# Attention before a routed MLP: three float32 key tiles per pair of heads instead of four

## The chip, the core and the metric

The kernel runs on one core of a Trainium2 chip. A core has TensorE (PE, matrix products; its weight loads are shown as PEld), VectorE (DVE), ScalarE (ACT), GpSimd (POOL) and SyncE (SP, which issues DMAs), each with its own instruction stream; they meet in semaphores. The metric is the time of one execution in microseconds; the median of three timed runs of the kernel before is 759.37 us (758.96 to 760.9).

## What is computed

Four batches of eight heads attend over 1152 keys with head size 64; the queries are first averaged in pairs, so there are 576 per head. The result goes through a routed MLP with eight experts (one per token, with a rule that keeps the previous token's expert for some tokens).

```python
q_pool = q.reshape(B, H, S // 2, 2, D).mean(axis=3)          # 4, 8, 576, 64
scores = scale * np.matmul(q_pool, k.transpose(0, 1, 3, 2))
attn = np.exp(scores - np.max(scores, axis=-1, keepdims=True))
attn = attn / (np.sum(attn, axis=-1, keepdims=True) + 1e-09)
x = np.matmul(attn, v)                                       # then the heads side by side
e = argmax(x[b, s] @ w_gate)  # or the token's before, where the local gate says so
out[b, s] = softmax(x[b, s] @ w_gate)[e] * (np.maximum(x[b, s] @ w1[e], 0.0) @ w2[e])
```

Everything is float32 from outside. Inside, most products are made of float16 or bfloat16 high and low parts.

## The kernel before

**Steps.** The 32 heads form 16 pairs (here numbered 0 to 15). A head has nine key tiles of 128 keys, so a pair has 18 steps; step `s` of the kernel is head `s // 9`, key tile `kt = s % 9`. The main loop in `attention` runs once per step and issues, in this order: `scores(s)` (four matmuls and, on ScalarE, the exponential into `PHI`, float32), `feed_max` (one or two units that compute the row maxima of the next head: matmuls into PSUM tiles tagged `m`, of which there are two, and a VectorE reduction, L199), one pending preparation operation of a later pair (`prep_ops`), at even steps `low(s // 2 - 1)`, and then `av(s - 6)`, since `LAG` is 6. So the value product of step 4 of a pair is issued in step 10 of the same pair.

**The value product.** `av(s)` multiplies the exponentials of one key tile with the values. For most tiles it takes three float16/bfloat16 products for each of five query blocks (L263 to L265): the top half of the float32 exponential (`top`, a bfloat16 view) with the high and with the low part of the values, and the low part of the exponential (`PLO`) with the high part of the values: 15 matmuls. For key tiles 4 and 8 (`F32K`) of each head it multiplies float32 with float32 instead (L261), five matmuls in the program, ten records in the trace, and needs no low part.

**Low parts.** `low(g)` computes `PLO` for two steps: POOL subtracts for the even step, VectorE for the odd one (L237). It leaves out the float32 tiles. POOL therefore makes the low parts of steps 0, 2, 6, 10, 12, 14 and 16 of a pair and VectorE those of 1, 3, 5, 7, 9, 11 and 15.

**Value tiles.** `VT` holds high part, a column of ones and low part in float16 for the seven tiles that are not float32; `VX` holds the two float32 tiles. `o6` makes the high parts with two ScalarE operations (L159, four tiles and three tiles for both heads), `o7` the low parts with two POOL operations (L162).

**What else runs in these steps.** From step 30 on, every 14 steps a piece of the experts' weights is loaded, converted by ScalarE and split by VectorE (`extra`; the split, L510, comes at steps 40, 54, 68 and so on). After every fourth pair a batch is finished; its router's many small VectorE operations come mainly in the steps of pairs 6, 10 and 14. After a head's last value product, ScalarE scales the result (L1171, L1165) and POOL subtracts once more (L1168, `xr`). All engines work through their own instructions in the order of the program. The order is the one in which the loop above issues them.

## Time and profile before

| | us |
|---|---|
| timed runs, median (lowest, highest) | 759.37 (758.96, 760.9) |
| the profiled execution | 763.41 |
| its span, first to last instruction | 761.4 |
| TensorE busy | 697.4 (92%) |
| VectorE busy | 620.5 (81%) |
| GpSimd busy | 503.4 (66%) |
| ScalarE busy | 477.0 (63%) |

The attention steps run from about 25 to 460 us, the experts after that. Busy shares are means over stages that have different limits, so what a change in the attention steps is worth has to be read in those steps: which engine waits for which there, and for how long. A timeline's row gives start, duration, engine, line and operation; a bracket at its end says how long the engine was idle before it and what it had waited for. A row of windows gives, for each stretch, how much of it each engine was busy, the granted share of TensorE's clock, and what the DMAs moved.

### The profile page before, as it was taken

What the parts mean: (1) busy time and instruction counts of PE and PEld (TensorE: products, weight loads), DVE (VectorE), ACT (ScalarE), POOL (GpSimd) and SP (SyncE); (2) the same over time, 40 slices, a digit from 0 to 9 for tenths busy, and PEclk for the clock granted to TensorE, in tenths of its full rate; (3) what the DMA queues carried; (4) which work ended last, traced back from release to release, by engine and by line L of the source; (5) the groups of instructions that cost most, each with busy time, mean ns of one, the idle gap of its engine ahead of it and who ended that gap; (6) DMA issues with size and microseconds to landing.
All of it is one profiled execution on the core that took longest, in us unless ns stands there. A gap on an engine that the chain in (4) does not pass through costs nothing. (4 is left out here: it accounts for less than half of the span.)

```text
span 761.4 us, 25799 instructions
## 1 busy us (share of the span) xinstructions
PE 697.4 (92%) x10664; PEld 611.1 (80%) x10664; DVE 620.5 (81%) x1098; ACT 477.0 (63%) x971; POOL 503.4 (66%) x456
## 2 busy tenths in 40 slices
PE   3899999999999999889999998888898999999994
PEld 0487788887778877778887887888897889999994
DVE  7778888888888888888888976689889899798851
ACT  2475777677477667567766655686767675565521
POOL 6575687778367767458666435853647567777776
PEclk9999999999899999999999999999999999999998
DMA  7363643586363586354593226696828884474411
GB/s 241 97 180 121 186 119 109 160 212 154 140 187 81 166 192 169 112 174 102 153 202 72 72 31 173 219 308 214 286 93 280 279 288 165 148 230 145 127 40 32
DMA packets 90058, 122.99 MB, mean 162 GB/s; under 512 B 40552, under 2 KB 46828, under 8 KB 89936
## 3 DMA queue, kind: packets, MB, share of 16 engines
q1 hardware_dynamic: 85152, 110.41, 49.8%
q0 software_dynamic: 4784, 10.86, 4.3%
q8 instruction: 87, 1.43, 0.8%
q14 instruction: 35, 0.29, 0.1%
HBM read 79.29 MB, written 16.85 MB: 126 GB/s over the span
## 5 line engine op out<-in xcount | busy, mean ns | idle before, releaser
L227 ACT ACTIVATE ph<-sc 128x576 f32<-128x576 f32 x288 | 187.6, 652 | 118.3 <-PE sc L225 99.8
L199 DVE TENSOR_REDUCE mx<-psm 128x1 f32<-128x512 f32 (+1 forms) x300 | 193.7, 662 | 57.2 <-PE psm L197 54.9
L237 POOL TENSOR_TENSOR pl<-ph 128x576 f16<-128x576 f32 x112 | 150.2, 1342 | 43.5 <-ACT ph L227 43.5
L934 DVE COPY wc<-w 128x2048 f16 x184 | 154.4, 839 | 26.7 <-PE pso L1069 22.6
L1061 PEld LDWEIGHTS <-wc 128*128 128x128 f16 x2208 | 126.1, 98 | 20.8 <-DVE wc L934 12.1
L264 PE MATMUL av<-vt,ph 128*128 128x64 f16 x1120 | 126.9, 196 | 0.0
L263 PE MATMUL av<-vt,ph 128*128 128x65 f16 x1120 | 126.4, 193 | 0.0
L265 PE MATMUL av<-vt,pl 128*128 128x65 f16 x1120 | 126.1, 192 | 0.0
L1069 PE MATMUL pso<-wc,hq 128*128 128x128 f16 x2208 | 123.4, 219 | 0.0
L1069 PEld LDWEIGHTS <-hq 128*128 128x128 f16 x2208 | 123.3, 98 | 0.0
L264 PEld LDWEIGHTS <-ph 128*128 128x128 bf16 x1120 | 104.9, 98 | 20.1 <-issue 0.5
L1073 POOL DMA_INDIRECT out<-ob,sid x92 | 100.6, 1093 | 30.9 <-issue 18.0
L225 PE MATMUL sc<-qa,ks 65*128 65x288 f16 (+1 forms) x576 | 119.9, 290 | 0.3 <-ACT qa L213 0.3
L263 PEld LDWEIGHTS <-ph 128*128 128x128 bf16 x1120 | 106.2, 98 | 17.2 <-issue 9.6
L223 PE MATMUL sc<-qs,ks 128*128 128x288 f16 x576 | 119.7, 290 | 0.2 <-ACT ph L227 0.2
L237 DVE TENSOR_TENSOR pl<-ph 128x576 f16<-128x576 f32 x112 | 106.3, 949 | 1.9 <-ACT ph L227 1.9
L265 PEld LDWEIGHTS <-pl 128*128 128x128 f16 x1120 | 105.3, 100 | 0.0
L508 POOL TENSOR_TENSOR w<-wf,w 128x512 f16<-128x512 f32 x48 | 62.8, 1315 | 53.4 <-ACT w L501 52.9
L197 PE MATMUL psm<-ks,qs 128*128 128x512 f16 x248 | 91.1, 387 | 6.6 <-DVE mx L199 6.1
L261 PEld LDWEIGHTS av<-vx,ph 128*128 128x128 f32 x640 | 82.1, 194 | 8.6 <-issue 5.1
L1168 POOL TENSOR_TENSOR xr<-xf,xr 128x320 f16<-128x320 f32 x30 | 33.2, 1106 | 77.1 <-ACT xr L1165 77.1
L1061 PE MATMUL psh<-xr,wc 128*128 128x128 f16 x1248 | 76.1, 221 | 8.7 <-DVE wc L934 5.8
(201 smaller groups left out, 1112.5 us busy)
## 6 DMA issues: line engine op xcount, KB each, us to landing
wf<-wq SPq DMA_DIRECT2D x128, 256.0 KB
qf<-qeo SPq DMA_DIRECT2D x16, 576.0 KB
vf<-vL SPq DMA_DIRECT2D x16, 576.0 KB
ks<-kd SPq DMA_DIRECT2D x32, 288.0 KB
kf<-kT SPq DMA_DIRECT2D x15, 576.0 KB
xts<-xr SPq DMA_DIRECT2D x23, 256.0 KB
qs<-qh SPq DMA_DIRECT2D x64, 72.0 KB
ks<-kl SPq DMA_DIRECT2D x32, 144.0 KB
```

Of the source, the lines that this page charges most:

```text
L199: V.tensor_reduce(out=mx[:, i, c:c + 1], in_=m[:, 0:w], op=ALU.max, axis=AX.X)
L223: T.matmul(sc[:, c, 0:288], ksl, QS[p][:, j, c * 288:(c + 1) * 288], start=True, stop=False)
L225: T.matmul(sc[:, c, 0:288], kal, QA[p % 3][u, j, c * 288:(c + 1) * 288], start=False, stop=True)
L227: A.activation(out=PHI[g % NPH][:, r * Q:(r + 1) * Q].rearrange("p (c q) -> p c q", c=2), in_=sc[:, :, 0:288], func=AF.Exp, scale=1.0 / 16)
L237: x.tensor_tensor(out=PLO[g % NPH][:, r * Q:r * Q + Q], in0=pf, in1=top(pf), op=ALU.subtract)
L263: T.matmul(o, ph[:, c:c + 128], v[:, j, kv, 0:65], start=(kt == 0 and t == 0), stop=False, skip_group_check=True)
L264: T.matmul(o[:, 0:64], ph[:, c:c + 128], v[:, j, kv, 65:129], start=False, stop=False, skip_group_check=True)
L265: T.matmul(o, pl[:, c:c + 128], v[:, j, kv, 0:65], start=False, stop=(kt == NKT - 1 and t == 4), skip_group_check=True)
L934: self.nc.vector.tensor_copy(w, self.W[ph % 2][:, bass.ds(self.ej[j], 1), :].rearrange("p o f -> p (o f)"))
L1061: self.nc.tensor.matmul(p[:, ft], w[:, ws, kk, ft * 128:ft * 128 + 128], x[:, 2 * kk + xs_], start=(n == 0 and ft == 0), stop=(n == 11 and ...
L1069: self.nc.tensor.matmul(p, h(hs, ft), w[:, ws, ft], start=(n == 0), stop=(n == 23))
L1073: sc = self.nc.gpsimd.indirect_dma_start(out=self.out.rearrange("b s (q d) -> (b s q) d", q=4), in_=o, in_offset=None, bounds_check=NTOK * ...
```

## The change

`FK` lists, for the first and the second head of a pair, which key tiles are float32: only tile 8 for the first, 4 and 8 for the second. So tile 4 of the first head (step 4 of each pair) is multiplied in float16, in 15 matmuls. Its low part is due at an even step and is thus made by POOL. `VT` holds eight tiles instead of seven, all that can be float16 in either head; `o6` converts the eight in one operation, and the second operation of `o7` covers four tiles instead of three. `VX` and its loads stay as they are.

```diff
--- before.py
+++ after.py
@@ -24,6 +24,7 @@
 LEAD = 4
 SHD = 3
 F32K = (4, 8)
+FK = ((8,), (4, 8))
 PREP0 = 13
 
 ONES = 0.007826805114746094
@@ -46,8 +47,7 @@
     KSA = [pers.tile([128, 2, 2, S], F16, name=f"ks{i}") for i in (1, 2, 0)]
     KSA = KSA[2:] + KSA[:2]
     QA = [pers.tile([128, 2, Q], F16, name=f"qa{i}") for i in range(3)]
-
-    VT = [lat.tile([128, 2, NKT - 2, 130], F16, name=f"vt{i}") for i in range(3)]
+    VT = [lat.tile([128, 2, NKT - 1, 130], F16, name=f"vt{i}") for i in range(3)]
     VX = [lat.tile([128, 2, 2, 65], F32, name=f"vx{i}") for i in range(2)]
     QD = [pers.tile([128, 128], F16, name=f"qd{i}") for i in range(3)]
     MN = [pers.tile([128, 5, 65 - 64 * i], F16, name=f"mn{i}") for i in range(2)]
@@ -151,12 +151,11 @@
                 r = slice(64 * j, 64 * j + 64)
                 SP.dma_start(out=QA[i][r, j], in_=ql[r])
 
-        vk = [vf.rearrange("p h (t d) -> p h t d", d=D)[:, :, k] for k in (slice(0, 4), slice(5, 8))]
-        tk = [VT[i][:, :, k] for k in (slice(0, 4), slice(4, 7))]
+        vk = [vf.rearrange("p h (t d) -> p h t d", d=D)[:, :, k] for k in (slice(0, 4), slice(4, 8))]
+        tk = [VT[i][:, :, k] for k in (slice(0, 4), slice(4, 8))]
 
         def o6():
-            for x, v in zip(tk, vk):
-                A.activation(out=x[:, :, :, 0:64], in_=v, func=AF.Copy)
+            A.activation(out=VT[i][:, :, :, 0:64], in_=vf.rearrange("p h (t d) -> p h t d", d=D)[:, :, 0:8], func=AF.Copy)
 
         def o7(g):
             G.tensor_tensor(out=tk[g][:, :, :, 65:129], in0=vk[g], in1=tk[g][:, :, :, 0:64], op=ALU.subtract)
@@ -232,7 +231,8 @@
 
     def low(g):
         for r, x in enumerate((G, V)):
-            if (2 * g + r) % NKT not in F32K:
+            n, kt = divmod(2 * g + r, NKT)
+            if kt not in FK[n % 2]:
                 pf = PHI[g % NPH][:, r * Q:r * Q + Q]
                 x.tensor_tensor(out=PLO[g % NPH][:, r * Q:r * Q + Q], in0=pf, in1=top(pf), op=ALU.subtract)
 
@@ -253,16 +253,16 @@
             AV[n] = ps_a.tile([128, 512], F32, name="av", tag="av")
         a = AV[n]
         ph, pl = top(PHI[s // 2 % NPH]), PLO[s // 2 % NPH]
-        v, kv = VT[p % 3], kt - (kt > F32K[0])
+        v = VT[p % 3]
         for t in range(5):
             o = a[:, t * 65:t * 65 + 65]
             c = (s % 2) * Q + t * 128
-            if kt in F32K:
+            if kt in FK[j]:
                 T.matmul(o, PHI[s // 2 % NPH][:, c:c + 128], VX[p % 2][:, j, F32K.index(kt)], start=False, stop=(kt == NKT - 1 and t == 4), skip_group_check=True)
                 continue
-            T.matmul(o, ph[:, c:c + 128], v[:, j, kv, 0:65], start=(kt == 0 and t == 0), stop=False, skip_group_check=True)
-            T.matmul(o[:, 0:64], ph[:, c:c + 128], v[:, j, kv, 65:129], start=False, stop=False, skip_group_check=True)
-            T.matmul(o, pl[:, c:c + 128], v[:, j, kv, 0:65], start=False, stop=(kt == NKT - 1 and t == 4), skip_group_check=True)
+            T.matmul(o, ph[:, c:c + 128], v[:, j, kt, 0:65], start=(kt == 0 and t == 0), stop=False, skip_group_check=True)
+            T.matmul(o[:, 0:64], ph[:, c:c + 128], v[:, j, kt, 65:129], start=False, stop=False, skip_group_check=True)
+            T.matmul(o, pl[:, c:c + 128], v[:, j, kt, 0:65], start=False, stop=(kt == NKT - 1 and t == 4), skip_group_check=True)
         if kt == NKT - 1:
             x = emit_x(n, AV.pop(n), ps_m, wide)
             later.extend(x[0])
```

GpSimd's order around the second pair's first steps, before (L237 is `low`, L1168 the subtraction behind a finished head, L162 the low part of the values, L126 the next pair's queries):

```order
L237 TENSOR_TENSOR pl_153<-ph_148 128x576
L1168 TENSOR_TENSOR xr<-xf,xr 128x5x64
L162 TENSOR_TENSOR vt_136<-vf,vt_136 128x2x3x64
L237 TENSOR_TENSOR pl_149<-ph_144 128x576
L237 TENSOR_TENSOR pl_151<-ph_146 128x576
L1168 TENSOR_TENSOR xr<-xf,xr 128x5x64
L237 TENSOR_TENSOR pl_153<-ph_148 128x576
L126 TENSOR_TENSOR qf<-qf_859 128x576
```

and now (the lines of `prep_ops` have moved up by one in the file):

```order
L237 TENSOR_TENSOR pl_153<-ph_148 128x576
L1168 TENSOR_TENSOR xr<-xf,xr 128x5x64
L161 TENSOR_TENSOR vt_136<-vf,vt_136 128x2x4x64
L237 TENSOR_TENSOR pl_149<-ph_144 128x576
L237 TENSOR_TENSOR pl_150<-ph_145 128x576
L237 TENSOR_TENSOR pl_151<-ph_146 128x576
L1168 TENSOR_TENSOR xr<-xf,xr 128x5x64
L237 TENSOR_TENSOR pl_153<-ph_148 128x576
```

The low part of step 4 (`pl_150`) stands between those of steps 2 and 6, ahead of the head's `xr`.

TensorE's order at step 10 of the same pair, before (L197 is a unit of the maxima, L223 the next step's scores):

```order
L197 LDWEIGHTS qs
L197 MATMUL psm<-ks_129,qs 128x512
L261 MATMUL av<-vx_138,ph_145 128x65 x5
L223 LDWEIGHTS ks_128
L223 MATMUL sc<-qs,ks_128 128x288
```

and the end of the same place now, the last two of five query blocks:

```order
L263 LDWEIGHTS ph_145
L263 MATMUL av<-vt_135,ph_145 128x65
L264 LDWEIGHTS ph_145
L264 MATMUL av<-vt_135,ph_145 128x64
L265 LDWEIGHTS pl_150
L265 MATMUL av<-vt_135,pl_150 128x65
L263 LDWEIGHTS ph_145
L263 MATMUL av<-vt_135,ph_145 128x65
L264 LDWEIGHTS ph_145
L264 MATMUL av<-vt_135,ph_145 128x64
L265 LDWEIGHTS pl_150
L265 MATMUL av<-vt_135,pl_150 128x65
```

In place of five float32 products stand 15 pairs of weight load and matmul, and the first L265 of them waits for POOL's `pl_150`.

## Rows read from the trace of the kernel before

**Rows 1.** Timeline of TensorE, pair 3: start us, us, engine line operation.

```profile
118.33 0.41 PE L223 MATMUL sc<-qs,ks 128*128 128x288 f16 x2
...
119.04 0.19 PE L263 MATMUL av<-vt,ph 128*128 128x65 f16 x1
...
119.50 0.41 PE L223 MATMUL sc<-qs,ks 128*128 128x288 f16 x2
...
120.21 1.23 PE L261 MATMUL av<-vx,ph 128*128 128x65 f32 x10
121.27 0.41 PE L223 MATMUL sc<-qs,ks 128*128 128x288 f16 x2
...
```

**Rows 2.** Windows, steps 10 to 13 of pairs 3, 4, 6, 15: length, busy per engine.

```profile
core 0: us, PE busy (x) PEld busy (x) DVE busy (x) ACT busy (x) POOL busy (x), PEclk, DMA share, GB/s
...
120.20:125.20 5.00, 5.00 (x77) 4.32 (x76) 4.49 (x7) 3.46 (x7) 3.86 (x4) 1.00 0.00 0
145.19:150.19 5.00, 4.69 (x67) 3.87 (x66) 5.00 (x8) 2.54 (x5) 3.87 (x3) 1.00 0.29 56
...
203.72:208.72 5.00, 5.00 (x77) 4.32 (x76) 4.79 (x9) 3.01 (x6) 3.86 (x4) 1.00 0.33 85
...
449.43:454.43 5.00, 5.00 (x79) 4.63 (x78) 2.65 (x6) 3.88 (x8) 3.52 (x3) 1.00 0.25 46
...
```

**Rows 3.** Timeline of VectorE (DVE), pair 3, then pair 4 from 146.67.

```profile
112.72 1.42 DVE L237 TENSOR_TENSOR pl<-ph 128x576 f16<-128x576 f32 x1
...
115.53 0.74 DVE L237 TENSOR_TENSOR pl<-ph 128x576 f16<-128x576 f32 x1
...
117.86 1.29 DVE L199 TENSOR_REDUCE mx<-psm 128x1 f32<-128x512 f32 x2 [0.48 <-PE psm L197]
...
122.17 2.07 DVE L199 TENSOR_REDUCE mx<-psm 128x1 f32<-128x512 f32 x3 [0.41 <-PE psm L197]
...
127.03 1.26 DVE L510 SCALAR_TENSOR_TENSOR w<-wf,w 128x512 f16<-128x512 f32 x1
...
146.67 1.28 DVE L510 SCALAR_TENSOR_TENSOR w<-wf,w 128x512 f16<-128x512 f32 x1
147.87 1.87 DVE L199 TENSOR_REDUCE mx<-psm 128x1 f32<-128x512 f32 x3
...
```

**Rows 4.** Timeline of TensorE, its waits for VectorE in pairs 4 and 6.

```profile
148.60 0.38 PE L197 MATMUL psm<-ks,qs 128*128 128x512 f16 x1 [0.31 <-DVE mx L199]
...
212.00 0.44 PE L212 MATMUL psh<-ident,mn 128*65 128x128 f16 x5 [0.39 <-DVE mx L199]
...
```

**Rows 5.** Groups by line and shape: names, count, busy us, mean ns, idle before.

```profile
L237 POOL TENSOR_TENSOR pl<-ph 128x576 f16<-128x576 f32 x112 | 150.2, 1342 | 43.5 <-ACT ph L227 43.5
...
L162 POOL TENSOR_TENSOR vt<-vf,vt 128x512 f16<-128x512 f32 x16 | 18.1, 1129 | 18.0 <-ACT vt L159 18.0
...
L162 POOL TENSOR_TENSOR vt<-vf,vt 128x384 f16<-128x384 f32 x16 | 15.7, 982 | 0.0
...
L159 ACT ACTIVATE vt<-vf 128x512 f16<-128x512 f32 x16 | 10.2, 635 | 1.1 <-DMA vf<-vL 1.1
...
L159 ACT ACTIVATE vt<-vf 128x384 f16<-128x384 f32 x16 | 8.4, 526 | 0.0
...
```

**Rows 6.** Timeline of GpSimd (POOL), pair 3.

```profile
113.48 1.67 POOL L237 TENSOR_TENSOR pl<-ph 128x576 f16<-128x576 f32 x1
115.64 1.64 POOL L237 TENSOR_TENSOR pl<-ph 128x576 f16<-128x576 f32 x1 [0.49 <-ACT ph L227]
121.34 1.08 POOL L1168 TENSOR_TENSOR xr<-xf,xr 128x320 f16<-128x320 f32 x1 [4.06 <-ACT xr L1165]
...
```

**Rows 7.** Waits from 60 to 460 us: total us, times, longest us.

```profile
POOL xr L1168 <- ACT xr L1165: 77.1, 16, 8.5
DVE mx L199 <- PE psm L197: 46.5, 79, 1.7
...
```

**Rows 8.** Windows, a stretch of pair 6; PEclk is the granted clock.

```profile
191.80:198.60 6.80, 6.80 (x46) 5.11 (x45) 4.79 (x13) 1.98 (x5) 1.09 (x1) 0.50 0.29 108
...
```

## What the change should do to the time

> **What bounds the kernel now.** I began with the waits of the attention stretch (60 to 460 us), went on to the timeline of TensorE in an undisturbed pair of heads, then to VectorE and GpSimd (POOL below) in the same microseconds, and last to one table that shows the same 5 us of all 16 pairs.
>
> The pairs are numbered 0 to 15, the 18 steps of a pair 0 to 17; step 4 is the one that is changed, and `av(4)` is issued in step 10. In pair 3 TensorE's steps follow each other without a gap [rows 1]. A step with a float16 block takes 1.17 us (118.33 to 119.50), a step with a float32 block 1.77 us (119.50 to 121.27). The float16 block itself is 15 matmuls between 119.04 and 119.50, a start every 0.031 us, 0.46 us in all; the float32 block is 10 records from 120.21 to 121.27, 1.06 us. So **a block that goes from float32 to float16 is worth 0.60 us of TensorE**, although it has more matmuls.
>
> The table of all pairs covers the 5.00 us from the start of exactly this block (step 10) [rows 2]. TensorE is busy 5.00 of 5.00 us in 13 of 16 pairs; in pairs 4, 8 and 11 it is 4.69, 4.91 and 4.69, and there VectorE is busy 5.00. So TensorE is the bound in most pairs at this place, and VectorE in some. The waits say the same [rows 7]: VectorE waited 46.5 us in 79 places for TensorE's maxima, POOL 77.1 us in 16 places for ScalarE.
>
> **The change part by part.**
>
> *TensorE.* One block of each pair changes, 16 in all: 16 x 0.60 = 9.6 us of TensorE. That is the most the change can give through this engine; what arrives depends on whether VectorE can follow, pair by pair.
>
> *Who is late next: VectorE.* After the block TensorE goes on with maxima, which VectorE reduces out of two PSUM buffers; where VectorE never idles between the block and TensorE's next wait for it, a faster TensorE only waits longer.
> - Nine pairs (0, 1, 2, 3, 5, 7, 9, 12, 13) look like pair 3: VectorE busy 4.29 to 4.50 of 5.00 [rows 2], idle 0.41 us before 122.17 because it waits for TensorE [rows 3]. Of the 0.60 us it can follow about 0.5 at once, and the second PSUM buffer lends the remaining 0.1 until its next idle time. I take 0.60 for seven of them (0.5 is the lower bound). In pairs 3 and 7 a weight split (L510, 1.26 us at 127.03 in pair 3 [rows 3]) comes soon after and uses that reserve up: 0.5 each.
> - Pairs 4, 8 and 11 have the L510 step near the block: VectorE is busy 5.00 [rows 2], in pair 4 with L510 at 146.67 and three maxima in a row at 147.87 [rows 3], and TensorE waits 0.31 us for it at 148.60 [rows 4]. A block that ends 0.60 us earlier makes this wait 0.91 us: gain 0.
> - Pairs 6, 10 and 14 also carry the router's small VectorE operations: 4.79 of 5.00, and the missing 0.21 lies before the block. In pair 6 TensorE then waits 0.39 us at 212.00 [rows 4]. Gain 0 again.
> - Pair 15 has no maxima left to compute (VectorE 2.65 of 5.00 [rows 2]): 0.60.
>
> Sum: 8 x 0.60 + 2 x 0.5 + 6 x 0 = **5.8 us**.
>
> *POOL's new subtraction.* Step 4 of each pair gets a low part, 16 x 1.34 us = 21.5 us of POOL [rows 5]. It stands between the low parts of steps 2 and 6. In pair 3 these start at 113.48 and 115.64 (the second one after waiting 0.49 us for step 6's exponential), then POOL idles 4.06 us until 121.34, waiting for ScalarE's output of the head before [rows 6]. The new operation's input is older than step 6's, so it starts at about 115.15 and is done by 116.8; TensorE needs it where the block starts, at 120.21 [rows 1]: 3.4 us to spare. Step 6 ends up to 1.67 us later, near 119, and is needed two steps after step 4. All of it is paid from the 4.06 us of idle time; without that cover each pair would lose up to 1.34 us. Cost 0.
>
> *The lock between POOL and VectorE.* Their two-input operations slow each other in the rows: VectorE's low part took 0.74 us at 115.53 but 1.42 us at 112.72, where POOL was in an operation already [rows 3]. The new POOL operation (about 115.15 to 116.5) will now stand across VectorE's low part at 115.53 and add up to 0.68 us to it. Behind it VectorE idles 0.48 us before 117.86 [rows 3] and some before that, so in ordinary pairs I take 0, with 0.68 as the upper bound. The Trainium skill, page "SBUF — State Buffer", section "Who interferes with whom", states this as a rule: the shared port pair is an exclusive lock, taken by whoever starts first, and the other one blocks fully. The trace agrees as far as 0.74 against 1.42 us goes.
>
> *The value tiles.* ScalarE's conversion becomes one operation of 1024 elements in place of 512 and 384 (0.635 and 0.526 us [rows 5]); it costs between 0.64 and 1.16 us, and I take 1.1, no change, by the sum of the two it replaces. POOL's first value subtraction now waits for the whole conversion instead of its first half, up to 0.5 us later, and its second one grows from 384 to 512 elements, 0.982 to 1.129 us [rows 5], 0.15 us a pair. Queued behind it are POOL's low parts of steps 0 and 2; in pair 3 the latter starts at 113.48 and would start 0.65 later, while TensorE reaches `av(2)` two steps ahead of 120.21, at about 117.9. Cost 0. The DMAs are the same (both float32 copies of values are still loaded).
>
> **The rivals.**
>
> *VectorE lets everything through.* If the pairs I set to 0 recover their share, the whole 9.6 us arrive: 749.8 us. For it: TensorE is busy 5.00 of 5.00 also in pairs 6, 10 and 14 [rows 2]. Against it: the waits at 148.60 and 212.00 [rows 4].
>
> *The lock eats a part.* In five pairs the new operation falls on a VectorE that has no idle time behind it: the router's pairs 6, 10 and 14, and pairs 5 and 12, where the code puts the weight split L510 into step 6. At 0.68 us each that is 3.4 us less: gain 2.4, 757.0 us; at half of it, 755.3. Against it: POOL's operations also move away from others.
>
> *VectorE bounds everywhere.* If the 0.5 us of idle time in the nine pairs turns out to be needed (for order, not for time), only pair 15 gains: 0.6 us, 758.8 us, no change. For it: VectorE is 4.49 of 5.00 busy. Against it: it is VectorE that waits there, for TensorE [rows 3, 7].
>
> *The clock: slower than before.* The waits of TensorE that grow in pairs 4, 8 and 11 (to about 0.9 us) and in 6, 10 and 14 could bring TensorE to half clock. In pair 6 it ran at a granted 0.50 from 191.80 to 198.60 [rows 8]; at half clock 6.8 us do the work of 3.4. One such stretch more leaves 2.4 us of the gain, two take it away, three make 3 x 3.4 - 5.8 = 4.4 us of loss: 763.8 us. Against it: the waits of 0.31 and 0.39 us [rows 4] were followed by no drop of the clock, and the gain is lost only from the second stretch on.
>
> *The float16 block isn't shorter.* If its 15 matmuls came at the pace of the float32 records (1.06 / 10 = 0.106 us) they would take 1.59 us, 0.53 more than now, 16 x 0.53 = 8.5 us of loss: 767.9 us. The even point is 1.06 / 15 = 0.071 us. Against it: the same 15 matmuls stand at 0.031 us in the step before [rows 1]. The Trainium skill speaks against this change here: page "TensorE: Matmul & The Clock Gate", section "Back-to-back issue gap", gives about 81 ns for each pair of weight load and matmul with 128 columns in a stream; by that figure 15 of them would be an estimated 1.2 us and the kernel about 2.4 us slower. The trace does not agree: 31 ns here, with 64 and 65 columns.
>
> **How the numbers follow.** The profiled execution took 763.41 us (span 761.4), 4.0 above the median of the three timed runs, 759.37; the sum is made against it (763.41 - 5.8 = 757.6), and since it consists of gaps that repeat in every pair I carry it to the median: 759.37 - 5.8 = **753.6 us**. Chances: this forecast (gain 4.2 to 7.2, 752.2 to 755.2) 0.58; everything arrives (down to 749.8) 0.11; the lock eats a part (755.2 to 757.0) 0.16; VectorE bounds everywhere 0.09; the clock 0.05; the pace of the block 0.01. The range of 8 in 10 leaves out the last three and the far end of the second: 750.5 to 757.0. A measurement of this kernel can tell 0.3% from no change, 2.3 us: faster 0.58 + 0.11 + 0.16 = 0.85, same 0.09, slower 0.06.
>
> **What would show it.** In the new profile step 10 of an ordinary pair should take 1.17 us on TensorE, its group of float32 matmuls count 480 instead of 640, and POOL have 128 low parts with its waits for ScalarE shorter by about 20 us. The table of the 5 us after the block should show VectorE at 5.00 in more pairs. In pairs 4, 8 and 11 TensorE's wait for VectorE should be 0.6 us longer, and nowhere should TensorE wait for POOL. Wrong would be: waits of TensorE for POOL's low part; half-clock stretches in pairs that had none; a step 10 that is short while the steps behind it grow by as much in ordinary pairs as well.

## The result: 0.6% slower instead of 0.8% faster

The changed kernel takes 766.88 us (median of 20 runs, 19 of them at 762.21 to 770.18), the kernel before in the same comparison 761.09 us (20 runs, 755.89 to 765.55): ratio 1.006, 95% interval 1.004 to 1.008, some 4.6 us slower. Medians here and below are over all runs, and ratios leave out slow ones, among them one of 2377.61 us of the changed kernel, one of 872.79 us of e_last_f32 and the profiled one of a_nolow (771.23 us). The forecast was 753.6 us, its range 750.5 to 757.0: wrong, and on the other side. The profiled executions are 763.41 us before and 766.23 us after, so the traces hold 2.8 us of the difference.

The page of the changed kernel: busy time of each engine with its share of the span and instructions, and three groups (line, engine, operation, count | busy us, mean ns | idle time before). Lines moved up by one around the maxima and the scores, so L198 is L199 of before, L196 is L197, L194 is L195, L222 is L223, L161 is L162 and L158 is L159:

```profile
span 764.2 us, 25974 instructions
PE 692.1 (91%) x10744; PEld 602.3 (79%) x10744; DVE 638.0 (83%) x1098; ACT 477.7 (63%) x955; POOL 529.4 (69%) x472
...
L237 POOL TENSOR_TENSOR pl<-ph 128x576 f16<-128x576 f32 x128 | 176.1, 1383 | 18.9 <-ACT ph L226 18.9
L237 DVE TENSOR_TENSOR pl<-ph 128x576 f16<-128x576 f32 x112 | 125.2, 1118 | 1.6 <-ACT ph L226 1.6
L196 PE MATMUL psm<-ks,qs 128*128 128x512 f16 x248 | 92.1, 390 | 13.6 <-DVE mx L198 12.5
```

TensorE's busy time fell by 5.3 us, POOL's rose by 26.0 and VectorE's by 17.5 with not one instruction more: its 112 low parts went from 949 to 1118 ns. Step 10 itself does what it should. TensorE in pair 3, starts of steps 10, 11 and 12 (against [rows 1]):

```profile
117.99 0.41 PE L222 MATMUL sc<-qs,ks 128*128 128x288 f16 x2
...
119.15 0.41 PE L222 MATMUL sc<-qs,ks 128*128 128x288 f16 x2
...
120.54 0.41 PE L222 MATMUL sc<-qs,ks 128*128 128x288 f16 x2
```

Step 10 takes 1.17 us instead of 1.77 here and in every other pair: 16 x 0.60 = 9.60 us less, with 15 matmuls at 0.031 us each in the block. The windows over the 5.00 us from the changed block on, pairs 3, 4, 6 and 15 (against [rows 2]):

```profile
core 0: us, PE busy (x) PEld busy (x) DVE busy (x) ACT busy (x) POOL busy (x), PEclk, DMA share, GB/s
118.69:123.69 5.00, 5.00 (x87) 4.22 (x85) 5.00 (x7) 4.06 (x7) 3.87 (x4) 1.00 0.01 2
144.06:149.06 5.00, 4.08 (x72) 3.25 (x71) 5.00 (x8) 2.52 (x5) 3.86 (x3) 1.00 0.27 52
200.69:205.69 5.00, 4.57 (x82) 3.72 (x81) 4.80 (x8) 3.02 (x6) 3.87 (x4) 1.00 0.33 83
450.11:455.11 5.00, 5.00 (x88) 4.57 (x85) 1.95 (x7) 3.79 (x8) 3.62 (x4) 1.00 0.26 49
```

VectorE is now busy 5.00 of 5.00 in pair 3 as well (4.49 before), and in pairs 4 and 6 TensorE has dropped to 4.08 and 4.57. The waits of the stretch from 60 to 460 us (total us, times, longest us; against [rows 7]):

```profile
DVE mx L198 <- PE psm L196: 32.8, 61, 1.1
...
POOL pl L237 <- ACT ph L226: 16.9, 12, 3.2
...
PE psm L196 <- DVE mx L198: 11.4, 13, 1.9
...
PE psm L194 <- DVE mx L198: 6.6, 10, 1.8
```

Of before, VectorE's group of low parts and the two waits that answer to the last two rows:

```profile
L237 DVE TENSOR_TENSOR pl<-ph 128x576 f16<-128x576 f32 x112 | 106.3, 949 | 1.9 <-ACT ph L227 1.9
```

```profile
PE psm L197 <- DVE mx L199: 5.8, 9, 1.9
...
PE psm L195 <- DVE mx L199: 3.4, 3, 1.2
```

VectorE waits 13.7 us less for TensorE, and TensorE waits about twice as long for VectorE.

**Where the 9.60 us went.** A step's length is the distance of two successive first score matmuls (L222) on TensorE. The table adds up each kernel's differences to the kernel before, over all pairs, without the steps that ran at half clock in either of the two traces; each row is one trace, and steps that a kernel leaves alone agree with those of before to 0.02 us in most pairs. The last columns are the stretch from the end of TensorE's last value matmul (L261) to the router's first column sums (L651), 7.58 us before, and the time against the kernel before on the same chip.

| kernel | step 10 | 6 | 8 | 12 | 15, 16 | others | sum | exit, us | ratio [95%] |
|---|---|---|---|---|---|---|---|---|---|
| changed | -9.60 | +3.60 | +1.91 | +4.17 | +0.78 | +0.09 | +0.95 | 11.00 | 1.006 [1.004, 1.008] |
| a_nolow | -9.60 | +2.00 | +0.91 | +3.44 | +0.79 | -2.39 | -4.86 | 10.35 | 1.0014 [0.9971, 1.0058] |
| b_two_act | -9.61 | +0.84 | +1.85 | +3.32 | +0.76 | +1.16 | -1.68 | 10.28 | 1.0026 [0.9991, 1.006] |
| c_vt_only | 0.00 | +2.30 | +0.93 | 0.00 | -0.07 | -1.18 | +1.98 | 7.58 | 1.0042 [0.9997, 1.0087] |
| d_low_only | 0.00 | +0.75 | +1.17 | 0.00 | -0.41 | -1.15 | +0.36 | 7.58 | 0.9999 [0.9954, 1.0044] |
| e_last_f32 | -9.01 | +3.11 | +1.91 | +3.31 | +0.78 | +0.45 | +0.55 | 7.58 | 1.0022 [0.999, 1.0054] |
| f_pairs | -3.00 | -0.19 | +0.42 | 0.00 | -0.04 | -0.77 | -3.58 | 9.74 | 1.0023 [0.9995, 1.0051] |
| g_sum | -9.01 | +0.10 | +0.47 | +4.18 | +0.77 | -1.22 | -4.71 | 8.36 | 0.9934 [0.9896, 0.9972] |
| h_split | -9.61 | +0.76 | +0.01 | +1.74 | -2.08 | -1.59 | -10.78 | 10.24 | 0.9854 [0.980, 0.9907] |
| l_before_slots | 0.00 | -2.11 | +0.03 | -0.93 | -2.52 | -4.01 | -9.54 | 7.58 | 0.9898 [0.984, 0.9955] |
| m_best_again | -9.01 | -1.41 | +0.01 | +1.48 | -1.19 | -2.42 | -12.55 | 7.58 | 0.9853 [0.9795, 0.9911] |

In the changed kernel steps 6, 8, 12 and 15/16 take back 10.46 us of the 9.60 gained, and the exit adds 3.4. Of the 4.17 us in step 12, 0.87 stands in pair 0; only g_sum and m_best_again show it again, and what makes it is open. The "others" are mostly single steps of up to 2 us beside the half-clock stretches and in pairs 0, 6, 10 and 14; I don't read them.

### The profile page after: what moved, and what is told of

The parts are those of the page before. It is cut to its first block, busy times and chain, and to the rows that moved or that the text cites. A ratio compares the mean times of both kernels' runs of the same rounds, so it can differ in the third digit from the quotient of the medians.

```text
span 764.2 us, 25974 instructions
## 1 busy us (share of the span) xinstructions
PE 692.1 (91%) x10744; PEld 602.3 (79%) x10744; DVE 638.0 (83%) x1098; ACT 477.7 (63%) x955; POOL 529.4 (69%) x472
## 5 line engine op out<-in xcount | busy, mean ns | idle before, releaser
L198 DVE TENSOR_REDUCE mx<-psm 128x1 f32<-128x512 f32 (+1 forms) x300 | 192.8, 660 | 41.5 <-PE psm L196 40.6
L237 POOL TENSOR_TENSOR pl<-ph 128x576 f16<-128x576 f32 x128 | 176.1, 1383 | 18.9 <-ACT ph L226 18.9
L1061 PEld LDWEIGHTS <-wc 128*128 128x128 f16 x2208 | 127.7, 99 | 17.3 <-DVE wc L934 8.3
L263 PEld LDWEIGHTS <-ph 128*128 128x128 bf16 x1200 | 113.7, 98 | 28.9 <-issue 21.4
L264 PE MATMUL av<-vt,ph 128*128 128x64 f16 x1200 | 136.1, 196 | 0.0
L263 PE MATMUL av<-vt,ph 128*128 128x65 f16 x1200 | 135.5, 193 | 0.0
L265 PE MATMUL av<-vt,pl 128*128 128x65 f16 x1200 | 135.2, 192 | 0.0
L264 PEld LDWEIGHTS <-ph 128*128 128x128 bf16 x1200 | 112.5, 98 | 22.1 <-issue 0.8
L237 DVE TENSOR_TENSOR pl<-ph 128x576 f16<-128x576 f32 x112 | 125.2, 1118 | 1.6 <-ACT ph L226 1.6
L1069 PE MATMUL pso<-wc,hq 128*128 128x128 f16 x2208 | 123.4, 219 | 0.0
L1069 PEld LDWEIGHTS <-hq 128*128 128x128 f16 x2208 | 123.3, 98 | 0.0
L1073 POOL DMA_INDIRECT out<-ob,sid x92 | 100.6, 1093 | 31.1 <-issue 17.7
L222 PE MATMUL sc<-qs,ks 128*128 128x288 f16 x576 | 119.6, 290 | 0.2 <-ACT ph L226 0.2
L265 PEld LDWEIGHTS <-pl 128*128 128x128 f16 x1200 | 112.9, 100 | 0.0
L196 PE MATMUL psm<-ks,qs 128*128 128x512 f16 x248 | 92.1, 390 | 13.6 <-DVE mx L198 12.5
L501 ACT ACTIVATE w<-wf 128x512 f16<-128x512 f32 x128 | 80.2, 628 | 3.0 <-DMA wf<-wq 1.3
L1168 POOL TENSOR_TENSOR xr<-xf,xr 128x320 f16<-128x320 f32 x30 | 28.4, 947 | 70.6 <-PE sc L224 64.6
```

The costliest lines, as they stand in the source:

```text
L198: V.tensor_reduce(out=mx[:, i, c:c + 1], in_=m[:, 0:w], op=ALU.max, axis=AX.X)
L222: T.matmul(sc[:, c, 0:288], ksl, QS[p][:, j, c * 288:(c + 1) * 288], start=True, stop=False)
L237: x.tensor_tensor(out=PLO[g % NPH][:, r * Q:r * Q + Q], in0=pf, in1=top(pf), op=ALU.subtract)
L263: T.matmul(o, ph[:, c:c + 128], v[:, j, kt, 0:65], start=(kt == 0 and t == 0), stop=False, skip_group_check=True)
L264: T.matmul(o[:, 0:64], ph[:, c:c + 128], v[:, j, kt, 65:129], start=False, stop=False, skip_group_check=True)
L265: T.matmul(o, pl[:, c:c + 128], v[:, j, kt, 0:65], start=False, stop=(kt == NKT - 1 and t == 4), skip_group_check=True)
```

## The experiments

The theory is that steps 12 and 15/16 are VectorE's (it cannot follow there), step 6 the value tiles', step 8 the new POOL operation's. The first four kernels take parts of the change away, or make one part alone.

**a_nolow**, the changed kernel without POOL's new low part from pair 1 on (these low parts are left out of the computation):

```diff
-            if kt not in FK[n % 2]:
+            if kt not in FK[n % 2] and not (n % 2 == 0 and kt == 4 and n):
```

> The changed kernel without GpSimd's low part of step 4 (from the second pair on; the 15 matmuls stay and multiply what an earlier step left in the buffer, so these low parts are left out of the result). Set against the kernel before, the changed kernel's trace has -9.6 us in step 10, and +3.6 in step 6, +1.9 in step 8, +4.2 in step 12, +1.7 in steps 15 and 16, summed over pairs. Theory LOCK (the new GpSimd operation delays VectorE's two-input operations): steps 6 and 8 come back to within 1 us of before, the sum of the attention steps is about 4 us under before. Theory VALUES (the merged ScalarE conversion and the longer GpSimd subtraction of the values shift GpSimd's queue against VectorE's): step 6 keeps its +3.6, only step 8 comes back, the sum is about 0 to -2 us. Both leave step 12 at +3 to +4, since VectorE is the bound there.

Measured: 763.55 us, before 762.69. Step 8 of pairs 5 and 12 falls from +0.85 and +0.84 to +0.18 and +0.20, and pair 15's +0.74 in step 6 goes. The +0.43 in step 6 of pairs 4, 5, 8 and 12 and the losses of six pairs in step 12 stay; the 0.87 of pair 0 does not. So the new subtraction costs, but not there. (The table has +0.78 for steps 15 and 16 where the expectation has +1.7: pair 10's 0.55 us is at half clock, and pair 14 is 0.41 us shorter.)

**b_two_act**, two ScalarE conversions of four tiles each for the value tiles:

```diff
-            A.activation(out=VT[i][:, :, :, 0:64], in_=vf.rearrange("p h (t d) -> p h t d", d=D)[:, :, 0:8], func=AF.Copy)
+            for x, v in zip(tk, vk):
+                A.activation(out=x[:, :, :, 0:64], in_=v, func=AF.Copy)
```

> The changed kernel with the values converted by two ScalarE operations of four tiles each instead of one of eight. Theory VALUES: step 6 loses most of its +3.6 us against before, the sum of the attention steps is 2 to 3.6 us under the changed kernel's. Theory LOCK: no change in step 6 or 8, the time stays at that of the changed kernel, about 0.6% over before.

Measured: 764.1 us. Step 6 goes back to 0 in pairs 4, 5, 8, 11 and 12 and to +0.24 in pair 2; pair 15's +0.74, which went with POOL's new low part in a_nolow, stays, and so do steps 8 and 12 of the other pairs. The merged ScalarE operation is what costs step 6 in the ordinary pairs.

**c_vt_only**, the kernel before with the value tiles of the change (`VT` of eight tiles, one ScalarE operation, POOL's second one of 512 elements) and `FK = ((4, 8), (4, 8))`, so four float32 tiles:

> The kernel before with the new value tiles alone: eight tiles, one ScalarE conversion, a GpSimd subtraction of four tiles; tile 4 of the first head stays float32. Theory VALUES: +2 to +3.6 us in step 6, nothing elsewhere; 0.3 to 0.5% slower than before. Theory LOCK: 0 within 0.5 us in the attention steps, same time as before.

Measured: 764.12 us. Step 6 shows +0.43 in pairs 4, 5, 8 and 12 and +0.68 in pair 9, with no other part of the change present (pair 2 ran at half clock there); step 8 shows 0.16 to 0.22 in pairs 1, 4, 5, 8 and 12, step 12 nothing.

**d_low_only**, the kernel before plus POOL's low part of step 4, which nobody reads:

```diff
-            if (2 * g + r) % NKT not in F32K:
+            if (2 * g + r) % NKT not in F32K or (2 * g + r) % (2 * NKT) == 4:
```

> The kernel before with GpSimd's low part of step 4 added for nobody: tile 4 stays float32 and does not read it. Theory LOCK: steps 6 and 8 grow by 2 to 5.5 us together, with step 10 unchanged: 0.3 to 0.7% slower. Theory VALUES: only step 8 grows, by about 1.9 us, 0.25% slower. Step 12 unchanged by either, since TensorE does not come earlier.

Measured: 762.97 us. +0.59 in step 8 of pairs 5 and 12, +0.75 in step 6 of pair 15, +0.13 in its step 9; steps 15 and 16 of pair 14 are 0.40 us shorter. The other named steps are as before. Where TensorE isn't earlier, POOL's 21.5 us of extra work cost what these steps show, and the time doesn't tell it from none.

How the value tiles reach TensorE is seen in pair 4. VectorE in steps 4 to 8 of before:

```profile
138.08 0.80 DVE L237 TENSOR_TENSOR pl<-ph 128x576 f16<-128x576 f32 x1
...
140.26 0.74 DVE L237 TENSOR_TENSOR pl<-ph 128x576 f16<-128x576 f32 x1
```

The same two low parts of VectorE in the changed kernel, then POOL's and TensorE's rows of these microseconds:

```profile
136.29 1.71 DVE L237 TENSOR_TENSOR pl<-ph 128x576 f16<-128x576 f32 x1
...
139.39 1.33 DVE L237 TENSOR_TENSOR pl<-ph 128x576 f16<-128x576 f32 x1
```

```profile
136.28 1.11 POOL L161 TENSOR_TENSOR vt<-vf,vt 128x512 f16<-128x512 f32 x1
137.35 4.38 POOL L237 TENSOR_TENSOR pl<-ph 128x576 f16<-128x576 f32 x3
```

```profile
138.66 0.22 PE L194 MATMUL psm<-kd,qd 128*128 128x128 f16 x1 [0.27 <-DVE mx L198]
...
147.49 0.38 PE L196 MATMUL psm<-ks,qs 128*128 128x512 f16 x1 [0.92 <-DVE mx L198]
```

POOL's second value subtraction starts at 136.28, 0.01 us ahead of VectorE's low part, which then takes 1.71 us; the maxima behind it are late, and TensorE waits in step 6. It stands there because POOL's first value subtraction before it waits for the merged conversion, 0.92 us, where it waited 0.50 us before (and 0.49 with two conversions), and POOL's operations behind it now meet VectorE's in another order. The first value subtraction in the changed kernel, then in the kernel before:

```profile
132.82 1.12 POOL L161 TENSOR_TENSOR vt<-vf,vt 128x512 f16<-128x512 f32 x1 [0.92 <-ACT vt L158]
```

```profile
133.91 1.13 POOL L162 TENSOR_TENSOR vt<-vf,vt 128x512 f16<-128x512 f32 x1 [0.50 <-ACT vt L159]
```

In c_vt_only, where only the value tiles are changed, VectorE and TensorE show the same picture:

```profile
139.37 1.71 DVE L237 TENSOR_TENSOR pl<-ph 128x576 f16<-128x576 f32 x1
```

```profile
141.73 0.22 PE L194 MATMUL psm<-kd,qd 128*128 128x128 f16 x1 [0.27 <-DVE mx L198]
```

In the kernel before POOL's second value subtraction is at 137.38, 0.70 us ahead of VectorE's low part, and ends soon behind its start:

```profile
137.38 0.88 POOL L162 TENSOR_TENSOR vt<-vf,vt 128x384 f16<-128x384 f32 x1
138.22 1.66 POOL L237 TENSOR_TENSOR pl<-ph 128x576 f16<-128x576 f32 x1
```

With two conversions it is at 135.52, again ahead of VectorE's by 0.71 us, and VectorE's takes 1.03 us:

```profile
135.52 1.12 POOL L162 TENSOR_TENSOR vt<-vf,vt 128x512 f16<-128x512 f32 x1
```

```profile
136.23 1.03 DVE L238 TENSOR_TENSOR pl<-ph 128x576 f16<-128x576 f32 x1
```

In step 8 of pair 5 the loss is in VectorE's low part ahead of the weight split. Both rows and TensorE's wait in the kernel before:

```profile
165.45 0.74 DVE L237 TENSOR_TENSOR pl<-ph 128x576 f16<-128x576 f32 x1
...
166.22 1.53 DVE L510 SCALAR_TENSOR_TENSOR w<-wf,w 128x512 f16<-128x512 f32 x1
```

```profile
168.40 0.38 PE L197 MATMUL psm<-ks,qs 128*128 128x512 f16 x1 [0.40 <-DVE mx L199]
```

The same in the changed kernel:

```profile
165.01 1.33 DVE L237 TENSOR_TENSOR pl<-ph 128x576 f16<-128x576 f32 x1
...
166.37 1.53 DVE L510 SCALAR_TENSOR_TENSOR w<-wf,w 128x512 f16<-128x512 f32 x1
```

```profile
168.55 0.38 PE L196 MATMUL psm<-ks,qs 128*128 128x512 f16 x1 [1.25 <-DVE mx L198]
```

L510 takes 1.53 us in both. The low part ahead of it, beside POOL's three (162.97 to 167.35 in the changed kernel), takes 1.33 us instead of 0.74, and TensorE's wait grows from 0.40 to 1.25. In d_low_only, where the new operation is the only change, the same low part takes 1.33 us, L510 1.53, and TensorE waits 0.99 us: 0.59 more, as its step 8 shows. The rest of the 0.85 us is of the size that c_vt_only shows in this step (0.19).

In a_nolow, without POOL's new operation, L510 itself is short, which it was not before:

```profile
169.35 0.65 DVE L510 SCALAR_TENSOR_TENSOR w<-wf,w 128x512 f16<-128x512 f32 x1
```

```profile
170.65 0.38 PE L196 MATMUL psm<-ks,qs 128*128 128x512 f16 x1 [0.58 <-DVE mx L198]
```

The next four ask about the exit, the sum of the causes, and the place of L510.

**e_last_f32**, the last pair kept at four float32 tiles:

```diff
+def f32_tiles(n):
+    return FK[n % 2] if n < 30 else F32K
...
-            if kt not in FK[n % 2]:
+            if kt not in f32_tiles(n):
```

> The changed kernel with the last pair (15) kept at four float32 key tiles. The theory (the exit from attention is lost because the last pair hands over early) expects that the stretch from the last product with the values to the router's first reduction returns from 11.0 us to about 7.6 us, that TensorE's wait at L567 for the DMA transposes (1.66 us) and the half-clock stretch at 466.5 us go, that pair 15's steps 6 and 10 stand as before (the 0.74 us lost in step 6 and the 0.60 us gained in step 10 both go), and 2 to 3 us less than the changed kernel: 763 to 764 us if the kernel before is again at 761 to 762. The rival (the exit is lost through the value tiles, or at random) expects 10 to 11 us there and a time within 0.7 us of the changed kernel.

Measured: 764.3 us, before 762.99. The exit is back at 7.58 us at full clock. By the ratios the time is some 3 us below the changed kernel's, as expected, but the intervals overlap. TensorE's rows there in the changed kernel, then windows over the exit of before, changed and e_last_f32 (the first number behind the length is TensorE's busy time, and 0.71 stands in the column of the granted clock):

```profile
461.74 0.25 PE L567 MATMUL psg<-wgh,xT 128*128 128x9 f16 x4
463.65 0.81 PE L567 MATMUL psg<-wgh,xT 128*128 128x9 f16 x26 [1.66 <-DMA xT<-xr]
```

```profile
461.82:469.40 7.58, 6.30 (x129) 5.35 (x125) 5.38 (x19) 4.20 (x7) 3.75 (x6) 1.00 0.89 289
```

```profile
461.90:472.90 11.00, 8.46 (x130) 7.54 (x125) 5.90 (x21) 3.98 (x7) 3.79 (x6) 0.71 0.73 239
466.50:473.30 6.80, 6.41 (x72) 5.74 (x71) 3.62 (x16) 3.02 (x6) 1.16 (x2) 0.50 0.61 214
```

```profile
464.69:472.27 7.58, 6.29 (x128) 5.35 (x124) 5.38 (x19) 4.20 (x7) 3.74 (x6) 1.00 0.90 280
```

The router needs five DMA transposes. Their first issue lies 10.18 us ahead of the end of TensorE's last value matmul before, and 9.60 us in the changed kernel, because pair 15's own block lies between the two and got 0.58 us shorter. The transposes got longer. SyncE's issues of them, before and in the changed kernel:

```profile
451.64 7.19 SPq L540 DMA_TRANSPOSE xT<-xr  x5
```

```profile
452.31 7.93 SPq L540 DMA_TRANSPOSE xT<-xr  x5
```

TensorE waits 1.66 us for them, and from 466.50 on it runs at a granted 0.50 for 6.80 us. The 0.58 us is thus only a part of the wait. The longest of the five issues takes 2.64 us in the changed kernel and 2.58 to 2.59 in a, b and h; with a float32 pair 15 it is 1.91 us before and 1.29 to 1.92 in c, d, e, f, g, l and m. In the changed kernel it is the fifth, with a packet of the instruction queue (q8) just ahead of it (457.4 to 457.7); before it is the fourth, with such a packet at 455.4 to 455.7. e_last_f32 takes away both the early hand-over and the long issue; which of them makes the wait was not tested.

Of the kernels on the chips where before takes some 762 us, all four with a float16 block in pair 15 (changed, a, b, h) have the wait and the clock stretch. Of those with a float32 one, before, c, d, e, l and m have neither, but g has a stretch of 3.4 us without a wait of TensorE above 0.31 us, and f waits 0.83 us for another DMA and has 6.8 us. So pair 15's block is one way into it and not the only one.

**f_pairs**, the change only in pairs 0, 1, 2, 9 and 13, two ScalarE conversions in all pairs:

```diff
+def f32_tiles(n):
+    return FK[n % 2] if n // 2 in (0, 1, 2, 9, 13) else F32K
...
```

> The change in pairs 0, 1, 2, 9 and 13 alone, where VectorE let the gain through, with two ScalarE conversions in every pair and POOL's second value operation at three tiles in the other pairs. The theory (the gain is kept wherever neither the weight split, the router nor the exit takes it back) expects 5 x 0.60 us less in step 10, up to 0.8 us of it lost in steps 6 of pairs 2 and 9, the exit from attention at 7.6 us as in the kernel before, and 2.2 to 3.0 us less than the kernel before. The rival (any lead of TensorE is taken back within a pair or two by VectorE) expects the sum of the steps within 1 us of the kernel before, and the same time.

Measured: 764.76 us against 762.99. The steps did what the theory says (-3.00 in step 10, 0 in step 12, -0.19 in step 6), the time did not: the exit took 9.74 us, and the trace has 30.6 us at half clock up to the end of the exit where the kernel before has 13.6; the profiled execution itself, at 761.15 us, was 2.3 us faster than that of before. Over its 12 runs the granted clock is 0.978, over the 27 runs of before 0.981. At this kernel's length 0.003 of the clock is an estimated 2.3 us, so a gain of 3 us in the steps is within reach of such shifts. The expected 2.2 to 3.0 us less did not come; why the clock is lower here is open.

**g_sum**, all suspected costs of the change away: e_last_f32 with two conversions and without POOL's new low parts (left out of the computation):

> The changed kernel with all suspected costs taken away together: pair 15 kept at four float32 tiles, two ScalarE conversions in place of the merged one, and no low part of key tile 4 of the first head from pair 1 on (these low parts are left out of the computation). If the causes are separate, step 10 gives 15 x 0.60 = 9.0 us, of which step 12 takes some 3.3 us and steps 15 and 16 some 1.2 us (VectorE is late there however the change is built), steps 6 and 8 stand within 0.5 us of the kernel before in every pair, and the exit is 7.6 us: some 4 us less than the kernel before, about what the prediction forecast. If the steps' losses only move elsewhere (VectorE bounds everywhere), the time is within 1 us of the kernel before.

Measured: 757.54 us, ratio 0.9934. Step 6 +0.10, step 8 +0.47, step 12 +4.18, steps 15/16 +0.77: the causes are separate, and what is left against the 9.01 us is mainly step 12 and steps 15/16, which follow the float16 block alone. The 5.4 us that this kernel gains (2.1 to 7.9 by the interval) is close to what I had forecast for the whole change, but it is reached without POOL's new low parts, so it isn't a gain that the change could have.

**h_split**, the changed kernel with the weight split three steps later in its cycle of 14:

```diff
-                if r == 10:
+                if r == 13:
                     m.w_lo(0, c, wt.pop(c), "V")
```

> The changed kernel with the weight split's subtraction (L510) put three steps later in its cycle of 14 steps, so that it falls in other pairs' step numbers (in pair 4 behind step 12 and not ahead of it; ahead of step 12 now in pairs 5 and 12). The theory that VectorE's work at L510 next to step 10 takes the gain back expects the 0.6 us lost in step 12 to vanish in pairs 4 and 11, to appear in pairs 5 and 12, and to stay in pairs 6, 10 and 14, where the router's work is the cause; the 0.6 us lost in steps 15 and 16 leave pairs 3 and 7 or change there. The rival (step 12 is short of VectorE's time by itself) expects the loss to stay in pairs 4 and 11. In the time as a whole no difference beyond 1 us from the changed kernel by either.

Measured: 752.8 us, ratio 0.9854. Step 12: pairs 4 and 11 go from +0.61 to -0.47, pairs 5 and 12 from 0 to +0.56, pairs 6, 10 and 14 stay at +0.59: the loss follows L510, as the theory says. Pair 3's step 16 goes from +0.60 to -0.25, pair 7's step 15 from +0.59 to -0.59. What no theory had is the rest: the steps together, half clock included, fall by 8.4 us against the changed kernel, many of them below the kernel before, and by the ratios the time is some 2% below the changed kernel's, where no difference beyond 1 us was expected.

The last runs ask what of that belongs to the tiles. The three that follow ran on another chip, on which the kernel before takes 798.33 us; only their ratios are compared.

**i_before_split**, the kernel before with that edit alone:

> The kernel before with one edit alone: the weight split's subtraction (L510) at step 13 of its cycle of 14 steps and not at step 10. The theory that L510 cost time in the kernel before already (it took 1.3 to 1.8 us there in most pairs, beside POOL, where 0.68 us is its time alone) expects the waits that it caused to go without any change of the key tiles: about 0.5 us each in steps 8 of pairs 5 and 12, steps 12 of pairs 4 and 11 and steps 15 or 16 of pairs 3 and 7, up to 0.9 us in step 6 of pairs 2 and 9: 3 to 5 us in all, 757 to 760 us if the kernel before is at 762, and the changed kernel with the same edit (752.8) lies below it by what the tiles bring. The rival (L510 is dear only when TensorE runs early, so that the edit brings back just what the change lost) expects no change: within 1 us of the kernel before.

Measured: 790.69 against 798.33 us, ratio 0.9901 [0.9863, 0.9938]. Steps -7.78 us, more than expected, and with four float32 tiles: L510 had cost time in the kernel before already.

**j_split_two**, h_split with two ScalarE conversions:

> The changed kernel with L510 at step 13 of its cycle and with two ScalarE conversions of the value tiles in place of the merged one. If the two causes are separate, the 0.43 us in step 6 of pairs 3, 4, 5 and 12 go as they did with two conversions alone, and the time is 1 to 2.5 us below the 752.8 us of the kernel with the moved subtraction alone: 750 to 752. If the moved subtraction has already taken the cause of step 6 away, the time is within 0.7 us of it.

Measured: 786.01 us, ratio 0.9839 [0.9788, 0.9891], against 0.9854 for h_split: not told apart. The 0.43 us in step 6 went in pairs 5 and 12 and stayed in pairs 3 and 4 (0.44 and 0.38), while pairs 11 and 13 now lose 0.37: two conversions take away a part of it here.

**k_best**, j_split_two with pair 15 at four float32 tiles and two chunks' splits four steps later still:

```diff
-                if r == 10:
-                    m.w_lo(0, c, wt.pop(c), "V")
+            for c in list(wt):
+                if s == 43 + 14 * c + 4 * (c in (4, 13)):
+                    m.w_lo(0, c, wt.pop(c), "V")
```

> As the run before it, and with two more edits: pair 15 kept at four float32 key tiles, and L510 four steps later still for the two chunks that would fall on step 9 of pairs 5 and 12. Expected of the first: the exit from attention at 7.6 us in place of some 10 us; of the second: the 0.56 us in step 12 of pairs 5 and 12 go. Together 2 to 4 us below the run with two ScalarE conversions: 747 to 749 us. If the exit's length does not hang on the last pair, about 1 us below it.

Measured: 783.57 us, ratio 0.9829 [0.9787, 0.9872]. That is 2.4 us below j_split_two, but the intervals overlap. Step 12 of pairs 5 and 12 is at 0.00, while step 15 of the same pairs grew by 0.4. Nothing can be read from the exit here: on this chip TensorE waits there for the DMAs with a float32 pair 15 as well (12.06 us in i_before_split).

**l_before_slots**, the kernel before with these places of L510, and **m_best_again**, k_best on the same chip beside it:

> The kernel before with L510 at the places of the fastest version (step 13 of its cycle, four steps later for the two chunks that fall on step 9 of pairs 5 and 12), four float32 key tiles in every pair. The theory that the moved subtraction gains by itself expects 6 to 8 us less than the kernel before on the same chip. The rival (it gains only together with the tiles) expects the kernel before's time within 2 us.

> The fastest version again, beside the run with its places of L510 and four float32 tiles, on one chip. The difference of the two is what the tiles bring once L510 is out of the way. The prediction's price (0.60 us a block, kept wherever VectorE lets it through, nothing in router pairs 6, 10 and 14) gives 12 x 0.60 = 7.2 us; with the 0.4 us that step 15 still lost in pairs 4, 5, 11 and 12 and the 0.4 us in step 6 of pairs 4, 11 and 3, 4 to 5 us. The rival (the tiles bring nothing even then) gives less than 1.5 us.

Measured: 752.78 and 751.28 us, before 762.45; ratios 0.9898 [0.984, 0.9955] and 0.9853 [0.9795, 0.9911]. L510 from 60 to 420 us, of before, of l_before_slots and of m_best_again (count | busy us, mean ns | idle before):

```profile
L510 DVE SCALAR_TENSOR_TENSOR w<-wf,w 128x512 f16<-128x512 f32 x16 | 21.6, 1351 | 0.0
```

```profile
L510 DVE SCALAR_TENSOR_TENSOR w<-wf,w 128x512 f16<-128x512 f32 x16 | 13.1, 817 | 0.0
```

```profile
L517 DVE SCALAR_TENSOR_TENSOR w<-wf,w 128x512 f16<-128x512 f32 x16 | 16.5, 1029 | 0.0
```

Most of the gain is L510's: l_before_slots, with four float32 tiles, has 1.0 of the 1.5%. The same 16 operations take 8.5 us less in their new places, and TensorE's wait for the maxima in l_before_slots falls from 5.8 to 2.2 us:

```profile
PE psm L197 <- DVE mx L199: 2.2, 5, 0.7
```

What the tiles add is 9.01 us in step 10, of which the steps keep 3.1 (step 12 takes 2.4, step 15 1.4, steps 6 and 7 0.7 each). That is below the 4 to 5 us expected. In the time the medians differ by 1.5 us and the means by 2.9, over six runs each that spread by 10 us: unclear. m_best_again is faster than the kernel before beyond its interval, and by the ratios than the changed kernel too; that the tiles have a share in it is not shown by the time.

## Why the prediction was wrong

Its sum was 9.6 us of TensorE minus 3.6 in six pairs without gain minus 0.2 in pairs 3 and 7.

- **0.60 us a block: right.** -9.60 us in step 10, 1.17 us, in all 16 pairs. The float32 records of L261 went from 640 to 480. The Trainium skill, "TensorE: Matmul & The Clock Gate", section "Back-to-back issue gap", gives its 81 ns for 128 columns. The estimate that carried them over to these blocks of 64 and 65 columns, where a start comes every 31 ns, does not hold.
- **No gain in pairs 4, 8, 11 and 6, 10, 14: right, but for pair 8, which kept half.** Their step 12 grows by 0.61, 0.32, 0.61, 0.59, 0.58 and 0.59. In pair 4 TensorE's wait went from 0.31 to 0.92 us, as forecast. h_split shows the cause: the loss moves from pairs 4 and 11 to 5 and 12 with L510 and stays in the router's pairs.
- **"0.5 each" in pairs 3 and 7: mis-sized.** Pair 3 gives back 0.60 us in step 16, pair 7 0.59 in step 15: gain 0. I let the L510 step of 1.26 us use up only the last 0.1.
- **POOL's new subtraction in time for TensorE: right.** TensorE never waits for a low part (L265).
- **"The value tiles ... Cost 0": the step that failed.** The merged ScalarE operation itself took 1.06 us, as I had it (1.1). But I costed only who waits for its data. POOL's value subtractions shifted against VectorE's low parts, and c_vt_only shows 2.30 us in step 6 and 0.93 in step 8 for the value tiles alone. The cover that I named, TensorE reaching the block two steps later, was real and beside the point: the lost time was VectorE's.
- **"In ordinary pairs I take 0, with 0.68 as the upper bound" for the lock: right for POOL's new low part in most pairs, wrong in 5, 12 and 15.** d_low_only shows 0.59, 0.59 and 0.75 us. This was the rival of the lock, in two of the five pairs that it named, plus pair 15. It did not occur to me that the value tiles set off the same lock, although the 1.42 us that I quoted from 112.72 stand beside a value subtraction, POOL's row of the kernel before:

```profile
112.64 0.89 POOL L162 TENSOR_TENSOR vt<-vf,vt 128x384 f16<-128x384 f32 x1
```

- **The gain passes on behind attention: failed, by an assumption I did not write down.** I carried a gain in the steps to the end of the kernel. With a float16 block in pair 15 the way to the router took 3.4 us longer, with a wait for the transposes and a stretch at half clock; that the early hand-over alone makes it is not shown. The rival of the clock had half clock as a cost right and the place wrong: no drop followed TensorE's waits of 0.92 us in pair 4 and 1.25 us in pair 5.
- **What would show it.** VectorE at 5.00 of 5.00 in nine pairs instead of three and POOL's waits for exponentials 23 us shorter (40.1 to 16.9) came. Of "wrong would be", growth behind a short step 10 came in pairs 3 and 7 alone, where it took the whole 0.60 us; most of the 5.5 us in steps 6 and 8 comes without a short step 10 too (c_vt_only, d_low_only). Half clock came in pair 9, which had none, though the attention steps as a whole had less of it (6.8 us instead of 13.6).

Of the 6.7 us between the forecast for the attention steps (-5.8) and the table (+0.95), 5.5 are steps 6 and 8, which the prediction had at nothing, and 1.2 are steps 12, 15 and 16, which lost 4.95 us where 3.8 were forecast. The exit comes on top.

The traces explain 2.8 us between the profiled executions: about 0 in the attention steps as a whole, +3.5 by L651, of which the experts give 1.8 back, and 1.1 more behind the last matmul (L1069). The medians differ by 5.8 us. The profiled execution of before was 2.3 us above its median, that of after 0.7 below; where the rest lies isn't shown.

## What to carry to other kernels

Before a step of the bound engine is made shorter, look at which engine follows it and what that engine does in the same microseconds: in 7 of 16 pairs a block that is 0.60 us shorter was worth nothing, and in an eighth half of it, because VectorE had an operation more to do there than TensorE's lead left time for. An operation that only changes its size or place on a side engine has to be laid over the other side engine's two-input operations, not only over those who wait for its data. And of work that can stand anywhere, such as a weight split, the place comes first: moving one operation by three steps was worth 1.0% of the time (0.9901 in i_before_split), an estimated 7.5 us at 762, more than the 5.8 that the tiles were to give.

## What the runs showed of the hardware

- **The lock holds VectorE until POOL's operation ends.** In pair 4 POOL's value subtraction ends at 138.26 us before, at 136.64 with two conversions and at 137.39 in the changed kernel; VectorE's low part ends 0.62, 0.62 and 0.61 us later (138.88, 137.26, 138.00), however early it started, so that it lasts 0.80, 1.03 or 1.71 us. L510 took 0.65 to 0.69 us alone and up to 1.77 beside POOL. VectorE's reductions, with one input that lies in PSUM, took 684 ns on average before and 682 after (60 to 420 us). The Trainium skill, "SBUF — State Buffer", section "Who interferes with whom", says that an operation of VectorE with two inputs in SBUF contends with POOL's reads and that a reduction does not on this chip. Both agree with these numbers, though a reduction that reads SBUF was not among them.
- **The half clock behind attention.** TensorE waited 1.66 us for a DMA until 463.65 and 0.52 us for ScalarE until 466.37, and from 466.50 on it ran at 0.50 (1.2 GHz) for 6.80 us; ten matmuls at L613 took 1.23 us there and 0.72 in the kernel before. Waits of 0.92 and 1.25 us within attention were not followed by a drop, and g_sum has 3.4 us at 0.50 behind attention with no wait above 0.31 us. What decides it was not found.
- **Chips differ.** On one of them the stage of L1069, whose code is the same in all kernels, took 144.8 us in i_before_split where the kernel before took 123.2 elsewhere, though TensorE's granted clock in that stretch was 1.00 on both. The scatters at L1073 took 1285 ns a piece there instead of 1093, but in j_split_two, on the same chip, they took 1076 and the stage was longer still, 156 us. TensorE itself started 463 matmuls from 630 to 660 us in i_before_split, 541 in the kernel before; the cause is open.
